# Cosine attention and a hard-swish layer in one kernel: batch 0's first two output tiles as a seven-product pair

## The chip, the cores and the metric

One core of one Trainium2 chip runs the kernel. The metric is device time in microseconds (us) for one execution; the kernel before takes 402.32 us (median of three runs, 402.19 to 402.92).

## The reference

The input is q, k, v of shape 8 batches x 12 heads x 448 positions x 64, and two weight matrices, 768 x 2048 and 2048 x 768.

```python
q_n = q / (norm(q) + 1e-06);  k_n = k / (norm(k) + 1e-06)      # over the last axis
attn = softmax(q_n @ k_n.T / tau)                              # tau = 0.1
x = (attn @ v), heads side by side: 3584 rows x 768
h = x @ w_in;  g = h * clip(h + 3, 0, 6) / 6
out = g @ w_out                                                # 3584 x 768, float32
```

## The kernel before, in words

The work is cut into 48 **turns**, one for each pair of heads of a batch (six turns a batch). A turn i has four groups of score matmuls (`SC.i.0` to `.2`, each two 64-row matmuls side by side, and `SC.i.3` on a tile `km`), an exponential on ScalarE for each bank of scores (`EX`), four groups of value matmuls into the bank pair `PV` (`VA`), and on VectorE a reciprocal and a multiplication that empty `PV` (`FI`). Ahead of a turn the raw q and k are loaded (`LQ`), squared (`SQ`), reduced (`RE`), scaled to `nrm` tiles (`NM`) and turned by a transposing DMA (`XD`); `CK` and `CS` copy the turned keys into `kz` (VectorE) and `km` (GpSimd); `VC` casts v into `vx`.

Between these, TensorE works through **units** of the layer (`U`). The first product, `mm1_unit(b, fc)` (L587), is six matmuls for one of 16 blocks of g; ScalarE makes `u` from it (`UA`, L596) and VectorE the product `gT` (`UV`, L602), which frees the bank. The second product, g @ w_out, comes in two forms. The plain one, `mm2_unit(b, t, m)` (L634), is 16 matmuls of 128x384 for one tile of 128 rows and one half of the columns. The other takes a **pair** of tiles and makes it with seven products of eight matmuls (`product_unit`, L795) in place of 4 x 16: products 1 to 7, named `x.n` for pair n. It needs sums of weight blocks (`WS`, L740: `w_sum` 1, 6 and 7, and `y3` and `y4`, which overwrite a quarter of `w_out_sb` each) and sums of blocks of g (`g_sum`, L772: `gs` tiles 6, 7, 1, and 2 and 5, which overwrite blocks of `gT`), all on VectorE. ScalarE copies out products 3, 4, 5 and 2; GpSimd combines the copies (`both`, `rest`, L824 to 828); VectorE adds product 1 into them (L852) and makes the results from 6 and 7 (L820).

The banks of scores, units and products come from one **ring of six** (M0, M1, Y, Z, M2, M3), handed out in program order. A matmul into a bank waits until the reader of what the bank held last has finished.

The order of the work is written by hand: `PLAN`, a list of operations for turns 0 to 17, whose `U` entries take units from `stream`; then a loop for turns 18 to 47, which takes them from `TURNS`, with the sums in `side`; then `LAST`. Each engine runs its own instructions in that order, and the DMAs of SyncE wait in one queue. `ORDER` lays out the stream of turns 8 to 17: 30 units of the first product, then six plain units of batch 0's second product. Two units of batch 1 (`carry`) are left for turn 18, and so is half of `y4`.

Of the kernel before, what the change touches and what calls it, by code (L numbers as in the profile page):

```python
# [15 lines left out]


FIRST = 18
ORDER = "111111111111111111111111111111222222"

PLAN = [
# [38 lines left out]
]  # L60

LAST = [
# [3 lines left out]
]  # L66
H_BY, M1_BY = "vvvvvvpp", "pppvpppp"

# [2 lines left out]
def kernel(  # L71
# [16 lines left out]
    NP = B * HP  # L88
    CC = d_model // 128
    FCN = d_ff // 128  # L90
# [22 lines left out]
    KC = FCN // 2  # L113
# [541 lines left out]
    def firsts(b, *fcs):  # L655
        return [(mm1_unit, b, fc) for fc in fcs]

    def second(b):
        assert b % 2 == 0
        return [(mm2_unit, b, t, m) for m in (1, 0) for t in range(3)]  # L660

    LEFT, RIGHT = slice(0, MH), slice(MH, 2 * MH)
    TILES = [(b, t) for b in range(1, B) for t in ((3, 0, 1, 2) if b % 2 else (0, 1, 2))]
    TILES.remove((B - 2, 2))
    PAIRS = list(zip(TILES[0::2], TILES[1::2]))  # L670
    ACROSS = [n for n, (x, y) in enumerate(PAIRS) if x[0] + 1 == y[0]]
    LOOP = 9
    summed, g_summed, issued_products = set(), set(), set()
    banks, parts, ready = {}, {}, set()
    late_sums = [
# [36 lines left out]
    def sum_of(n, what):  # L712

        if what == "e":
            return gs["1"] if n < B - 2 else late_sums[1]["e"]
        if n < LOOP or n == len(PAIRS) - 1:
            return gs[what + str(n % 2) if what == "7" else what]
        return late_sums[(n - LOOP) % 2][what]

    def d_and_e(n):  # L720
        if n < LOOP:
            return wide[n % 2], wide[2]
        return wide_late[2 * (n - LOOP) : 2 * (n - LOOP) + 2]

    def weight_sums(what, c0, n):
# [17 lines left out]
    def half(b, t, k):  # L743

        complete(b, t)
        return g_of(b)[:, :, g_cols(b, t)].rearrange("p (c k) n -> p c k n", k=2)[:, :, k, :]

    def block(n, i, k):
        return half(*PAIRS[n][i], k)

    def g_sum(n, what):

        if what == "e":
            t = 2 + n % 2
            o, x, y, op = sum_of(n, "e"), half(n, t, 0), half(n, t, 1), ALU.add
        else:
            a11, a12 = (block(n, 0, k) for k in range(2))
            a21, a22 = (block(n, 1, k) for k in range(2)) if what != "5" else (a11, a12)
            for w in {"2": "6", "5": "" if n in ACROSS else "7"}.get(what, ""):
                assert (n, w) in g_summed  # L760
            o, x, y, op = {
                "6": (a21, a21, a11, ALU.subtract),
                "2": (a21, a21, a22, ALU.add),
                "7": (a12, a12, a22, ALU.subtract),
                "5": (a12, a12, a11, ALU.add),
                "1": (a11, a11, a22, ALU.add),
            }[what]
            if what in "167":
                o = sum_of(n, what)
            if what == "5" and n in ACROSS:  # L770
                o = gs["6"]
        nc.vector.tensor_tensor(out=o[:, :, :], in0=x, in1=y, op=op)  # L772
        g_summed.add((n, what))

    def product_unit(n, name, end=None, apart=False):
# [54 lines left out]
        def added_later(i, cols, x):  # L830
# [230 lines left out]
    def sums(n, names):  # L1061
        return [(g_sum, n, x) for x in names]
# [16 lines left out]
    TURNS = {  # L1079
# [5 lines left out]
    }  # L1085
    APART = {(n, y) for n in range(len(PAIRS)) for x, y in (("5a", "3"), ("2a", "4")) if f"{x}.{n}" in " ".join(TURNS.values()).split()}
    side = {
        18: [(weight_sums, "y4", KC // 2, KC // 2)], 19: sums(0, "62"), 20: sums(0, "1"),
        21: sums(1, "75"), 22: sums(1, "621"),
        25: sums(2, "75"), 27: sums(2, "621"), 28: [(g_left, 2)], 29: sums(3, "5"),  # L1090
        31: sums(3, "7612"), 33: sums(4, "75"), 34: sums(4, "621"), 36: sums(5, "5"),
        37: sums(5, "761"), 38: sums(5, "2"), 39: [(g_left, 4)],
        40: sums(6, "75"), 41: sums(6, "621"),
        43: sums(7, "75"), 44: sums(7, "62"), 45: sums(7, "1"), 46: sums(8, "75"), 47: sums(8, "62"),
    }
    w_sums = [(w_sum_of, x, p) for p in range(FCN // 4) for x in "15672"]
    late = {44: "p", 45: "ppppp", 46: "pp"}
    units = {}
    carry = firsts(1, FCN - 2, FCN - 1)
    for b in range(2, B - 1):  # L1100
        first = firsts(b, *range(FCN))
        for n, x in enumerate([0, 3, 3, 3, 3, 2]):
            i = (b + 1) * HP + n
            u = carry + [first.pop(0) for _ in range(x)]
            carry = []
# [5 lines left out]
            if i == NP - 1:  # L1111
                p, last = [last], None
            x = 0 if n == 1 else 1 if n in (0, 5) and i > FIRST else 2
            units[i] = u[:x] + p + u[x:]
            units[i] += [last] if last else []
        carry = first
    units[FIRST] += sums(0, "75")

    assert len(carry) == 2
    units[NP] = [x for line in LAST for x in listed(line)]  # L1120
    units[NP] += products("3.10 4.10") + sums(10, "1") + products("5.10") + sums(11, "75") + products("2.10 3.11") + sums(11, "62")
    units[NP] += products("4.11 5.11") + sums(11, "1") + products("2.11 1.10 1.11")
    units[NP] += [(product_unit, n, x, 2) for n, x in ((10, "7"), (10, "6"), (11, "6"))]
    units[NP] += [(product_unit, 11, "7", x) for x in range(2)]

    FG = d_ff // 4
    weights = [
# [34 lines left out]
    def finish_units(e):  # L1162
        post[e].pop(0)()

    def whole_units(n, engines="av"):
# [6 lines left out]
    OPS = {  # L1172
        "LQ": load_qk, "LV": load_v, "W": next_weights, "SQ": square, "RE": reduce, "NO": norms, "NN": norms_two,
        "NM": normalise, "VC": vcast, "TR": transposes, "XD": crossbar, "XB": back_crossbar, "XP": back_two, "CQ": copy_q, "CK": copy_k, "CS": copy_k3, "SC": scores,
        "EX": exps, "VA": values, "FI": finish_values, "BK": back, "CX": copy_x, "U": unit, "UA": lambda: finish_units("a"), "UV": lambda: finish_units("v"),
        "GL": g_left, "WS": lambda x, *h: weight_sums(str(x), *((h[0] * KC // 2, KC // 2) if h else (0, KC))), "UU": whole_units, "D": busy, "DP": busy_pv, "OPEN": open_ring,
    }

# [31 lines left out]
    psum_s = startup.enter_context(tc.tile_pool(name="psum_s", bufs=1, space=bass.MemoryType.PSUM))  # L1210
    SC = [psum_s.tile([128, 2, 512], FP32, name=f"SC{n}", tag=f"SC{n}") for n in range(2)]

    by_kind = {"1": firsts(0, *range(FCN)) + firsts(1, *range(FCN - 2)), "2": second(0)}
    stream = [by_kind[x].pop(0) for x in ORDER]
    assert not by_kind["1"] and not by_kind["2"]


    for line in PLAN:
        run(line)
# [4 lines left out]
    for i in range(FIRST, NP):  # L1224
        assert not stream
        stream = list(units[i])
# [34 lines left out]
        n = 2  # L1261
# [27 lines left out]
    stream = units[NP]  # L1289
# [36 lines left out]
```

## Time and profile before

| what | us |
|---|---|
| median of the runs | 402.32 |
| the profiled execution's own time | 401.72 |
| its span, first to last instruction | 399.8 |
| TensorE matmul busy | 390.0 (98%) |
| VectorE busy | 296.1 (74%) |
| ScalarE busy | 281.6 (70%) |
| GpSimd busy | 266.8 (67%) |

In the page and the answers, PE is TensorE, DVE is VectorE, ACT is ScalarE, POOL is GpSimd, SP is SyncE. A timeline row has the start in us from the span's start, the length in us, the engine, the line, the operation with what it writes and reads, how many instructions are merged, and in brackets the idle time of the engine before the row with what ended it. The trace draws a matmul with its way through the array, so that rows of TensorE overlap; what a unit takes from the engine is the distance from its start to the start of the next row. The stretch that the change touches lies between 91 and 122 us.

### The profile page before, as it was taken

To read this page: it belongs to the slowest core of one execution; us is meant where nothing else is said; L and a number is where in the kernel's file an instruction comes from. 1 tells how busy PE (TensorE), PEld (TensorE's weight loads), DVE (VectorE), ACT (ScalarE), POOL (GpSimd) and SP (SyncE) were. 2 spreads that over 40 slices of the span, in tenths; PEclk is the share of its full clock that TensorE was granted. 3 is DMA by queue.
4 is the path that set the end of the run, shared out by engine and by line. 5 is a ranking of instruction groups with operands and counts; after the bars stand their busy time and mean duration, and the time that the engine had idled before them with its cause. 6 is when DMAs were issued, how large, how long until landed. Compare 5 with 4: busy or idle time off the path is not lost.

```text
span 399.8 us, 9819 instructions
## 1 busy us (share of the span) xinstructions
PE 390.0 (98%) x3735; PEld 238.3 (60%) x3735; DVE 296.1 (74%) x537; ACT 281.6 (70%) x619; POOL 266.8 (67%) x257
## 2 busy tenths in 40 slices
PE   7998999999999999999999999999999999999996
PEld 5566556555665556555565565555555556687563
DVE  7998787877588777767667796677856676888863
ACT  6999889887377686788788678776758755265330
POOL 5899936753544996578668888379395893344270
PEclk9999999999999999999999999999999999999999
DMA  8999999798878558797879787976763523130133
GB/s 290 317 232 243 198 206 246 167 201 188 193 165 217 122 116 196 198 207 147 197 184 215 98 205 152 163 186 154 185 152 74 112 48 58 34 77 21 39 82 97
DMA packets 93166, 63.75 MB, mean 159 GB/s; under 512 B 56128, under 2 KB 93120, under 8 KB 93120
## 3 DMA queue, kind: packets, MB, share of 16 engines
q1 hardware_dynamic: 87408, 56.45, 61.5%
q0 software_dynamic: 5312, 6.29, 9.7%
q8 instruction: 29, 0.48, 0.6%
q10 hardware_dynamic: 400, 0.39, 0.3%
q14 instruction: 17, 0.14, 0.1%
HBM read 45.61 MB, written 11.01 MB: 142 GB/s over the span
## 4 chain that ended last, share of the span: by engine, by line
PE 84%; ACT 5%; DMA 3%; DVE 3%; SPq 2%; POOL 2%; issue 1%; ACTq 0%; DVEq 0%; POOLq 0%
PE M L587 20%; PE M L795 17%; PE PV L482 10%; PE Z L587 6%; PE M L442 5%; PE Y L587 5%; PE Y L795 5%; PE Z L795 4%; PE M L634 3%; ACT at L460 3%; DMA big<-in_q_dram 2%; PE M L954 2%; PE Y L442 1%; PE Z L442 1%; SPq L219 1%
## 5 line engine op out<-in xcount | busy, mean ns | idle before, releaser
L460 ACT ACTIVATE at<-M 128x448 bf16<-128x448 f32 x196 | 98.1, 564 | 19.4 <-PE M L442 16.6
L587 PEld LDWEIGHTS <-w_in_sb 128*128 128x128 bf16 x696 | 65.2, 98 | 56.5 <-issue 2.8
L587 PE MATMUL M<-xT,w_in_sb 128*128 128x448 bf16 x450 | 96.7, 352 | 0.2
L293 POOL TENSOR_TENSOR nrm<-big,r 128x896 bf16<-128x896 f32 (+1 forms) x47 | 78.5, 1675 | 11.3 <-DMA tT<-nrm 4.2
L236 POOL TENSOR_TENSOR big<-big 128x896 f32<-128x896 f32 (+5 forms) x45 | 68.7, 1533 | 17.3 <-DMA big<-in_k_dram 8.8
L482 PEld LDWEIGHTS <-at 128*128 128x128 bf16 (+1 forms) x1536 | 54.1, 97 | 19.9 <-issue 12.0
L602 DVE SCALAR_TENSOR_TENSOR gT<-u,M 128x448 bf16<-128x448 bf16 x71 | 43.2, 618 | 30.7 <-ACT u L596 30.0
L482 PE MATMUL PV<-vx,at 128*128 128x65 bf16 (+1 forms) x1536 | 62.7, 193 | 0.0
L596 ACT ACTIVATE u<-M,bias 128x448 bf16<-128x448 f32 x75 | 49.0, 657 | 12.4 <-PE M L587 11.4
L248 DVE TENSOR_REDUCE n<-big 128x14 f32<-128x896 f32 (+1 forms) x50 | 51.5, 1038 | 0.3 <-ACT big L234 0.2
L399 POOL COPY km<-tT 64x128 bf16<-64x128 bf16 x34 | 15.6, 460 | 52.7 <-PE M L442 27.4
L795 PEld LDWEIGHTS <-gT 128*128 128x128 bf16 x304 | 29.5, 98 | 20.2
L795 PE MATMUL M<-w_out_sb,gT 128*128 128x384 bf16 x200 | 36.4, 326 | 0.0
L795 PEld LDWEIGHTS <-gs 128*128 128x128 bf16 x264 | 25.5, 98 | 17.5 <-issue 0.3
L503 DVE TENSOR_TENSOR on<-PV,rc 128x512 bf16<-128x512 f32 x48 | 33.2, 692 | 1.7
L795 PE MATMUL M<-w_sum,gs 128*128 128x384 bf16 (+1 forms) x184 | 32.0, 319 | 0.1
L442 PE MATMUL M<-tT,kz 64*128 64x448 bf16 (+1 forms) x171 | 31.0, 351 | 0.5 <-ACT at L460 0.5
L587 PE MATMUL Z<-xT,w_in_sb 128*128 128x448 bf16 x138 | 29.9, 353 | 0.0
L460 ACT ACTIVATE at<-Y 128x448 bf16<-128x448 f32 x50 | 28.3, 565 | 1.5 <-PE Z L442 1.5
L312 POOL CAST vx<-big 128x512 bf16<-128x512 f32 x39 | 27.1, 699 | 2.9 <-DMA big<-in_v_dram 2.8
L460 ACT ACTIVATE at<-Z 128x448 bf16<-128x448 f32 x48 | 27.1, 564 | 2.7 <-PE M L442 2.4
L587 PE MATMUL Y<-xT,w_in_sb 128*128 128x448 bf16 x108 | 23.4, 352 | 0.0
(163 smaller groups left out, 625.0 us busy)
## 6 DMA issues: line engine op xcount, KB each, us to landing
big<-in_k_dram SPq DMA_DIRECT2D x24, 448.0 KB, 5.2
big<-in_q_dram SPq DMA_DIRECT2D x24, 448.0 KB, 4.3
out_dram<-o SPq DMA_DIRECT2D x107, 96.0 KB, 2.2
big<-in_v_dram SPq DMA_DIRECT2D x48, 128.0 KB, 4.4
big<-in_v_dram SPq DMA_DIRECT2D x48, 96.0 KB, 4.5
w_in_sb<-in_moe_w_in_dram POOLq DMA_DIRECT2D x8, 384.0 KB, 9.3
w_out_sb<-in_moe_w_out_dram POOLq DMA_DIRECT2D x4, 768.0 KB, 10.0
tT<-nrm SPq DMA_TRANSPOSE x34, 2.8
```

What stands on the lines that cost most here:

```text
L236: engines[e].tensor_tensor(out=o, in0=i, in1=i, op=ALU.mult)
L248: nc.vector.tensor_reduce(out=n2_and_r[0][:, d % 2, j % 2, c], in_=sq[:, :, :, :].rearrange("p g c d -> p (g c) d")[:, c, :], axis=AX.X, o ...
L293: engines[e].tensor_tensor(out=nrm[:, :, g, :].rearrange("p c g d -> p g c d"), in0=raw_of[j][:, g, :, :], in1=n2_and_r[4][:, d % 2, j % 2, :]
L312: (engines[e].copy if e == "a" else engines[e].tensor_copy)(out=o, in_=f)
L442: nc.tensor.matmul(o, ks, qt[rows], start=True, stop=True)
L460: nc.scalar.activation(out=o, in_=x, func=AF.Exp, scale=inv_tau)
L482: nc.tensor.matmul(pv_out(j, h), at[rows, n, q_cols(i // HP, j)], vt[rows, 3 + h if name == "M" else 5 * h + int(name[1]), :], start=(name ...
L503: nc.vector.tensor_tensor(out=on[:, :, :, :].rearrange("p j h d -> p h j d"), in0=pv4[:, :, :, 0:D], in1=rc[:, :, :].to_broadcast([128, 2, ...
L587: nc.tensor.matmul(ps[:, 0:S], w_in_sb[:, cc, fc * 128 : (fc + 1) * 128], x[:, cc, 0:S], start=(cc == 0), stop=(cc == CC - 1),)
L596: nc.scalar.activation(out=u[:, :], in_=ps[:, 0:S], func=AF.Relu, bias=half_bias, scale=1.0 / 6.0)
L602: nc.vector.scalar_tensor_tensor(out=g[:, fc, c0 : c0 + S], in0=u[:, :], scalar=1.0, in1=ps[:, 0:S], op0=ALU.min, op1=ALU.mult,)
L795: nc.tensor.matmul(m, lhs[:, c, :], rhs[:, c, c0 : c0 + width], start=(base is None and c == 0), stop=(c == KC - 1), skip_group_check=True,)
```

## The change

The first two tiles of batch 0's second product, (0,0) and (0,1), become pair 0 of the seven-product form; the third, (0,2), stays plain. All later pairs are numbered one higher and keep their place. `PLAN`'s last lines are written anew for turns 15 to 17: the two left-over units of batch 1 come back into them from turn 18, the weight sums are all made before turn 17, the sums of g for pair 0 are set at three places (`GS`), and product 7 of pair 0 is put into turn 18. The results' stores move with the units; no load and no transposing DMA changes its place among the others in SyncE's queue. Pair 0 uses `wide[0]` and `wide[1]` for its two partial results.

The core of the diff:

```diff
 PLAN = [
...
-    "EX.14.3 XD.17 U SC.15.0 U FI.13 EX.15.0 UA UV UA UV UA U UA VA.14.0 VA.14.1 LQ.22 VA.14.2 UV UV CK.16.v VA.14.3",
+    "EX.14.3 XD.17 U SC.15.0 U FI.13 EX.15.0 SQ.20.p.0.7 GS.0.n62 UA UA VA.14.0 VA.14.1 LQ.22 LV.8 VA.14.2 VC.17.p",
...
     TILES.remove((B - 2, 2))
+    TILES[0:0] = [(0, 0), (0, 1)]
-    LOOP = 9
+    LOOP = 10
...
-            return wide[n % 2], wide[2]
+            return wide[n % 2], wide[2 if n else 1]
...
-        18: "3.0 4.0", 19: "5a.0 2a.0", 20: "1.0 6.0", 21: "3.1 5.1", 22: "4.1 2.1", 23: "1.1 6.1",
+        18: "7.0 3.1 4.1", 19: "5a.1 2a.1", 20: "1.1 6.1", 21: "3.2 5.2", 22: "4.2 2.2", 23: "1.2 6.2",
...
-        18: [(weight_sums, "y4", KC // 2, KC // 2)], 19: sums(0, "62"), 20: sums(0, "1"),
+        19: sums(1, "62"), 20: sums(1, "1"),
...
-    carry = firsts(1, FCN - 2, FCN - 1)
+    carry = []
...
+        "GS": lambda n, x: [g_sum(n, y) for y in x[1:]],
...
-    by_kind = {"1": firsts(0, *range(FCN)) + firsts(1, *range(FCN - 2)), "2": second(0)}
-    stream = [by_kind[x].pop(0) for x in ORDER]
+    stream = firsts(0, *range(FCN)) + firsts(1, *range(FCN - 2)) + [(mm2_unit, 0, 2, m) for m in range(2)]
+    stream += firsts(1, FCN - 2, FCN - 1) + products("4.0 2.0 3.0 5.0 1.0 6.0")
```

Line numbers of the changed kernel are one lower up to L634 and nine lower from L740 on (L772 is its L763).

**VectorE behind the emptying of `PV` for turn 13**, before. The rows are the reciprocal and the multiplication of `FI.13`, four products `gT` of the first product's units (each frees the bank named behind `u`), and the copy of the keys of turn 16:

```order
L502 RECIPROCAL rc_1604<-PV_109 128x8
L503 TENSOR_TENSOR on_1409<-PV_109,rc_1604 128x2x4x64
L602 SCALAR_TENSOR_TENSOR gT1_72<-u_1609,M1_695 128x448
L602 SCALAR_TENSOR_TENSOR gT1_72<-u_1612,Y_110 128x448
L602 SCALAR_TENSOR_TENSOR gT1_72<-u_1615,M3_697 128x448
L602 SCALAR_TENSOR_TENSOR gT1_72<-u_1623,M0_694 128x448
```

The same place in the changed kernel:

```order
L501 RECIPROCAL rc_1604<-PV_109 128x8
L502 TENSOR_TENSOR on_1409<-PV_109,rc_1604 128x2x4x64
L763 TENSOR_TENSOR gs6_77<-gT0_71 128x1024
L763 TENSOR_TENSOR gT0_71<-gT0_71 128x8x128
L601 SCALAR_TENSOR_TENSOR gT1_72<-u_1612,M1_695 128x448
L601 SCALAR_TENSOR_TENSOR gT1_72<-u_1614,Y_110 128x448
L601 SCALAR_TENSOR_TENSOR gT1_72<-u_1655,M3_697 128x448
L601 SCALAR_TENSOR_TENSOR gT1_72<-u_1657,M0_694 128x448
```

The sums 6 and 2 of pair 0 now stand ahead of the four products that free M1, Y, M3 and M0.

**VectorE from the keys of turn 16 on**, before: weight sums with a copy of keys, the plain units' stores (`o`) and the emptying of `PV` between them.

```order
L740 TENSOR_TENSOR w_sum7_75<-w_out_sb_68 128x1536
L740 TENSOR_TENSOR w_sum1_73<-w_out_sb_68 128x3072
L389 COPY kz1_81<-tT0_83 128x384
L647 COPY o_1796<-M1_695 128x384
L502 RECIPROCAL rc_1800<-PV_109 128x8
L503 TENSOR_TENSOR on_1663<-PV_109,rc_1800 128x2x4x64
L740 TENSOR_TENSOR w_sum6_74<-w_out_sb_68 128x3072
L647 COPY o_1838<-M2_696 128x384
L248 TENSOR_REDUCE n2_102<-big_94 128x14
L740 TENSOR_TENSOR w_out_sb_68<-w_out_sb_68 128x8x384
```

In the changed kernel; the first row that writes `w_out_sb` is `y4`, the second `y3`:

```order
L731 TENSOR_TENSOR w_sum7_75<-w_out_sb_68 128x1536
L731 TENSOR_TENSOR w_sum1_73<-w_out_sb_68 128x3072
L731 TENSOR_TENSOR w_out_sb_68<-w_out_sb_68 128x8x384
L731 TENSOR_TENSOR w_sum6_74<-w_out_sb_68 128x3072
L646 COPY o_1788<-M3_697 128x384
L601 SCALAR_TENSOR_TENSOR gT1_72<-u_1746,M0_694 128x448
L601 SCALAR_TENSOR_TENSOR gT1_72<-u_1753,M1_695 128x448
L731 TENSOR_TENSOR w_out_sb_68<-w_out_sb_68 128x8x384
L388 COPY kz1_81<-tT0_83 128x384
L763 TENSOR_TENSOR gs70_78<-gT0_71 128x1024
L763 TENSOR_TENSOR gT0_71<-gT0_71 128x8x128
L763 TENSOR_TENSOR gs1_76<-gT0_71 128x1024
```

Four weight sums now follow one another, `y3` comes behind the last two products of batch 1, and three sums of g follow.

**GpSimd in the same stretch**, before: the copies into `km` for turns 16 and 17, casts of v, the scaling `NM.18` and the squares of item 20.

```order
L399 COPY km_82<-tT0_83 64x2x64 x2
L312 CAST vx0_95<-big_94 128x8x64
L312 CAST vx1_96<-big_94 128x8x64
L293 TENSOR_TENSOR nrm0_99<-big_94,r_106 128x2x7x64
L312 CAST vx3_98<-big_94 128x8x64
L236 TENSOR_TENSOR big_94<-big_94 128x896
L312 CAST vx2_97<-big_94 128x8x64
```

In the changed kernel; L815, L816 and L819 combine the copies of pair 0:

```order
L235 TENSOR_TENSOR big_94<-big_94 128x896
L311 CAST vx1_96<-big_94 128x8x64
L292 TENSOR_TENSOR nrm0_99<-big_94,r_106 128x2x7x64
L311 CAST vx0_95<-big_94 128x8x64
L398 COPY km_82<-tT0_83 64x2x64 x2
L815 TENSOR_TENSOR big_94<-big_94 128x384
L816 TENSOR_TENSOR big_94<-big_94,o_1872 128x384
L311 CAST vx3_98<-big_94 128x8x64
L819 TENSOR_TENSOR big_94<-big_94,o_1812 128x384
```

The copies into `km` stand behind two casts and a scaling, and three additions are new.

TensorE's order from the end of turn 14's units, in words. Before: `mm1` into M0, the values of turn 14, scores 15.1 and 15.2 (M1, Y, Z, M2), 15.3 (M3), a plain unit (M0), values 15.0 and 15.1, all scores of turn 16 but the last, values 15.2 and 15.3, two plain units (M1, Y), scores 16.3, a plain unit (M2), values, scores 17.0 to 17.2, values, two plain units (M3, M0), scores 17.3 (M1), and turn 18 with two `mm1` and products 3 and 4. In the changed kernel: three groups of the values of turn 14, `mm1` (M0), the fourth group, scores 15.1 and 15.2 (M1, Y, Z, M2), the plain unit (M3), scores 15.3, 16.0 and 16.1, the other plain unit (M3), `mm1` twice (M0, M1), scores 16.2, product 4 (M2), values 15.0 to 15.2, scores 16.3 (M3), product 2 (M2), product 3 (M0), scores 17.0 and 17.1, values 15.3, product 5 (M0), product 1 (M3), values 16.0, scores 17.2, values 16.1 to 16.3, product 6 (M3), scores 17.3 (Y), values 17.0, and turn 18 with its scores (Z, M2, M3, M0, M1, Y), values, product 7 (Z), scores 18.3 and products 3 and 4 of pair 1.

More of the change, by code (lines that the diff above doesn't have):

```diff
@@ L18 @@
 FIRST = 18
-ORDER = "111111111111111111111111111111222222"
 PLAN = [
@@ L656, in firsts @@
         return [(mm1_unit, b, fc) for fc in fcs]
-    def second(b):
-        assert b % 2 == 0
-        return [(mm2_unit, b, t, m) for m in (1, 0) for t in range(3)]
     LEFT, RIGHT = slice(0, MH), slice(MH, 2 * MH)
@@ L1087 @@
     side = {
-        18: [(weight_sums, "y4", KC // 2, KC // 2)], 19: sums(0, "62"), 20: sums(0, "1"),
[L1089 to L1094, printed above, removed]
+        19: sums(1, "62"), 20: sums(1, "1"),
+        21: sums(2, "75"), 22: sums(2, "621"),
+        25: sums(3, "75"), 27: sums(3, "621"), 28: [(g_left, 2)], 29: sums(4, "5"),
+        31: sums(4, "7612"), 33: sums(5, "75"), 34: sums(5, "621"), 36: sums(6, "5"),
+        37: sums(6, "761"), 38: sums(6, "2"), 39: [(g_left, 4)],
+        40: sums(7, "75"), 41: sums(7, "621"),
+        43: sums(8, "75"), 44: sums(8, "62"), 45: sums(8, "1"), 46: sums(9, "75"), 47: sums(9, "62"),
     }
@@ L1116 @@
         carry = first
-    units[FIRST] += sums(0, "75")
+    units[FIRST] += sums(1, "75")
     assert len(carry) == 2
     units[NP] = [x for line in LAST for x in listed(line)]
[L1121 to L1124, printed above, removed]
+    units[NP] += products("3.11 4.11") + sums(11, "1") + products("5.11") + sums(12, "75") + products("2.11 3.12") + sums(12, "62")
+    units[NP] += products("4.12 5.12") + sums(12, "1") + products("2.12 1.11 1.12")
+    units[NP] += [(product_unit, n, x, 2) for n, x in ((11, "7"), (11, "6"), (12, "6"))]
+    units[NP] += [(product_unit, 12, "7", x) for x in range(2)]
     FG = d_ff // 4
@@ L1174 @@
         "NM": normalise, "VC": vcast, "TR": transposes, "XD": crossbar, "XB": back_crossbar, "XP": back_two, "CQ": copy_q, "CK": copy_k, "CS": copy_k3, "SC": scores,
-        "EX": exps, "VA": values, "FI": finish_values, "BK": back, "CX": copy_x, "U": unit, "UA": lambda: finish_units("a"), "UV": lambda: finish_units("v"),
+        "EX": exps, "VA": values, "FI": finish_values, "BK": back, "CX": copy_x, "U": unit, "UA": lambda: finish_units("a"), "UV": lambda: finish_units("v"), "UP": lambda: finish_units("p"),
+        "GS": lambda n, x: [g_sum(n, y) for y in x[1:]],
         "GL": g_left, "WS": lambda x, *h: weight_sums(str(x), *((h[0] * KC // 2, KC // 2) if h else (0, KC))), "UU": whole_units, "D": busy, "DP": busy_pv, "OPEN": open_ring,
@@ L1211 @@
     SC = [psum_s.tile([128, 2, 512], FP32, name=f"SC{n}", tag=f"SC{n}") for n in range(2)]
-    by_kind = {"1": firsts(0, *range(FCN)) + firsts(1, *range(FCN - 2)), "2": second(0)}
-    stream = [by_kind[x].pop(0) for x in ORDER]
-    assert not by_kind["1"] and not by_kind["2"]
+    stream = firsts(0, *range(FCN)) + firsts(1, *range(FCN - 2)) + [(mm2_unit, 0, 2, m) for m in range(2)]
+    stream += firsts(1, FCN - 2, FCN - 1) + products("4.0 2.0 3.0 5.0 1.0 6.0")
     for line in PLAN:
```

25 rows, old and new, of tables (LAST, PLAN, TURNS) are left out of this document.

## The prediction

> **What bounds the kernel now.** I read the page first, then the table by stretches, then the timelines of the four engines between 80 and 122 us, then places elsewhere where VectorE and GpSimd overlap.
>
> ```profile
> span 399.8 us, 9819 instructions
> PE 390.0 (98%) x3735; PEld 238.3 (60%) x3735; DVE 296.1 (74%) x537; ACT 281.6 (70%) x619; POOL 266.8 (67%) x257
> PE 84%; ACT 5%; DMA 3%; DVE 3%; SPq 2%; POOL 2%; issue 1%; ACTq 0%; DVEq 0%; POOLq 0%
> ...
> 92.20:121.47 29.27, 29.27 (x285) 18.08 (x284) 21.84 (x33) 18.25 (x41) 14.93 (x14) 1.00 0.76 172
> ```
>
> TensorE is busy 98% of the span and 84% of the chain that ended last. The last row is the stretch that is rewritten, from the `mm1` unit into M0 to the first values of turn 18: 29.27 us, TensorE busy throughout at its full granted clock (1.00), VectorE 21.84, GpSimd 14.93. So the end moves by what TensorE is spared there, less every wait put into its stream; behind the stretch its order is as it was.
>
> **What TensorE is spared.** A unit's price is the distance between starts:
>
> ```profile
> 88.39 1.30 PE L587 MATMUL M<-xT,w_in_sb 128*128 128x448 bf16 x6
> 89.53 1.30 PE L587 MATMUL Y<-xT,w_in_sb 128*128 128x448 bf16 x6
> 90.76 0.36 PE L442 MATMUL Z<-tT,kz 64*128 64x448 bf16 x1
> ...
> 91.06 2.44 PE L587 MATMUL M<-xT,w_in_sb 128*128 128x448 bf16 x12
> 93.34 1.14 PE L482 MATMUL PV<-vx,at 128*128 128x65 bf16 x32
> 94.41 0.36 PE L442 MATMUL M<-tT,kz 64*128 64x448 bf16 x1
> ...
> 118.87 2.76 PE L795 MATMUL M<-w_out_sb,gT 128*128 128x384 bf16 x16
> 121.47 0.63 PE L482 MATMUL PV<-vx,at 128*128 128x65 bf16 x16
> ```
>
> Sixteen matmuls of 128x384 take 121.47 - 118.87 = 2.60, so one takes 0.1625, not the 0.326 of its drawn length. Six plain units were 96 matmuls; now there are 32 and seven products of eight, 88. Eight fewer: **-1.30**. Against it, an `mm1` unit takes 1.14 in front of another (88.39 to 89.53) and 1.23 in front of scores (89.53 to 90.76): leaving or entering a group of 64-row scores costs 0.09. (The Trainium skill, "TensorEngine Tiling (Array Packing)", Key Properties, says that changing the tiling mode drains the engine; these rows agree, and the rule speaks against this order. Without the drain the sum would be 0.42 us lower.) Four groups of scores become six, three of them entered from 128-row work where all four came behind values: 2 x 0.09 + 0.24 = +0.42, the 0.24 being an estimate for the entries (0.1, 0.1 and 0.05 behind a `km` matmul). The values in eight pieces rather than seven come to +0.01. TensorE's own work: -1.30 + 0.42 + 0.01, about **-0.87**.
>
> **The sums ahead of the first four products.** VectorE had a hole there, which the sums 6 and 2 are to fill:
>
> ```profile
> 90.74 0.69 DVE L503 TENSOR_TENSOR on<-PV,rc 128x512 bf16<-128x512 f32 x1
> 92.69 0.62 DVE L602 SCALAR_TENSOR_TENSOR gT<-u,M 128x448 bf16<-128x448 bf16 x1 [1.26 <-ACT u L596]
> 93.23 0.61 DVE L602 SCALAR_TENSOR_TENSOR gT<-u,Y 128x448 bf16<-128x448 bf16 x1
> 93.76 1.15 DVE L602 SCALAR_TENSOR_TENSOR gT<-u,M 128x448 bf16<-128x448 bf16 x2
> ...
> 91.69 1.69 POOL L293 TENSOR_TENSOR nrm<-big,r 128x896 bf16<-128x896 f32 x1 [4.25 <-DMA tT<-nrm]
> ```
>
> Two sums of 0.68 would fit 1.26 with 0.1 over. But GpSimd starts `NM.19` at 91.69, when a transposing DMA lets go of its tile, and no edit touches that. What the two do to each other stands elsewhere:
>
> ```profile
> 233.24 0.91 DVE L772 TENSOR_TENSOR gs<-gT 128x1024 bf16<-128x1024 bf16 x1
> 234.19 2.06 DVE L772 TENSOR_TENSOR gT<-gT 128x1024 bf16<-128x1024 bf16 x1
> ...
> 233.56 2.14 POOL L293 TENSOR_TENSOR nrm<-big,r 128x896 bf16<-128x896 f32 x1
> ```
>
> The same three instructions: the scaling drawn from 233.56 waited for the first sum (to 234.15) and ran 1.55; the second sum, drawn from 234.19, waited for the scaling (to 235.70) and ended 0.55 later. They exclude each other, and the one that waits goes next. (The Trainium skill, "SBUF — State Buffer", Who interferes with whom, says that a VectorE instruction with two SBUF inputs contends with GpSimd's reads and that issue order decides who blocks. These rows agree and add the turn-taking. By that rule alone, with each wait in order of issue, the next step is the same.)
>
> So: sum 6 runs 91.35 to 92.03, `NM.19` to 93.58, sum 2 to 94.13. The four products then start at 94.05, 94.58, 95.11 and 95.64, the second ends at 95.19, and only then is Y free for scores 15.1. TensorE gets there at 94.42: from 92.20 (91.06 + 1.14) it has an `mm1`, 1.14, and the 32 values in two pieces, 1.08 (1.07 in one, 93.34 to 94.41). It then starts 0.05 behind the release, an estimate, at 95.24: **+0.82**. The plain unit's bank M3 (product ended 95.72) adds **+0.05**.
>
> **The weight sums ahead of product 3.** Lengths and the exclusion for these:
>
> ```profile
> 95.92 0.95 DVE L740 TENSOR_TENSOR w_sum<-w_out_sb 128x1536 bf16<-128x1536 bf16 x1
> ...
> 103.64 1.79 DVE L740 TENSOR_TENSOR w_sum<-w_out_sb 128x3072 bf16<-128x3072 bf16 x1
> 109.18 1.75 DVE L740 TENSOR_TENSOR w_out_sb<-w_out_sb 128x3072 bf16<-128x3072 bf16 x1
> ...
> 98.80 1.17 POOL L312 CAST vx<-big 128x512 bf16<-128x512 f32 x2 [2.84 <-DMA big<-in_v_dram]
> ...
> 103.76 2.14 POOL L312 CAST vx<-big 128x512 bf16<-128x512 f32 x1
> ```
>
> A cast of 0.61 took 2.14 beside the weight sum at 103.64, and ended 0.47 behind it. VectorE after the products, each of which takes its turn for 0.53 (92.69 to 93.23): the emptying for turn 14 from 96.17, keys at 97.02, `w_sum` 7 at 97.28, `w_sum` 1 at 98.14 to 99.89. The cast of v cannot start before 98.80 (its load, unmoved) and gets in at 99.89; `y4` follows to 101.98, `NM.18` to 103.53, `w_sum` 6 to 105.15. Then a store copy, two products and `y3`, 106.60 to 108.35, and GpSimd's second cast and the two `km` copies, 105.15 to 106.28.
>
> TensorE with the waits so far: scores 15.1 at 95.24, plain unit 95.77 to 98.37, scores 15.3, 16.0 and 16.1, second plain unit 99.10 (its bank's copy, 0.48 on ScalarE, ends 99.05: +0.01) to 101.70, two `mm1`, scores 16.2, product 4 from 104.35 to 105.65 (`y4` done at 101.98), values 15, scores 16.3 at 106.40 (`km` at 106.28: 0.1 to spare), product 2 to 107.89. Product 3 reads `y3`: 108.40, **+0.52**. Before, `y3` at 109.18 had ten us to spare.
>
> **The end of pair 0.**
>
> ```profile
> 120.43 0.48 ACT L843 COPY big<-M 128x384 f32<-128x384 f32 x1 [0.72 <-PE M L795]
> ...
> 102.32 0.56 DVE L647 COPY o<-M 128x384 f32<-128x384 f32 x1 [3.52 <-PE M L634]
> ...
> 110.84 1.16 DVE L236 TENSOR_TENSOR big<-big 128x512 f32<-128x512 f32 x2
> ...
> 134.00 1.00 POOL L825 TENSOR_TENSOR big<-big,o 128x384 f32<-128x384 f32 x1
> ```
>
> A copy starts 0.25 behind a product's end (118.87 + 1.30 to 120.43) and takes 0.48; a bank emptied by VectorE takes 0.56. Product 5 ends at 111.92, its copy at 112.65. GpSimd's subtraction (1.00) meets the two squares at 112.3, which I let exclude it: d is ready at 113.83, VectorE adds product 1 behind the second square, 114.16 to 114.71, and product 6, due at 114.59, starts at 114.76: **+0.17** (nothing if the squares don't exclude it, 0.6 if both go first). Turn 18's second scores need M3 from product 6's result: 116.06 + 0.25 + 0.55 + 0.05 = 116.91 against 116.79, **+0.12**; they replace a wait of **0.07** that the stretch has now for M1. Everything else of the change has cover: sums 7, 5 and 1 end at 110.54, just ahead of product 5 (110.62) and of product 1 (111.92); GpSimd's three new additions lie where it stood idle from 105.9 to 114.8; stores number as before; `XD.18` goes out at some 110.9 for 109.0, still ahead of its keys' copy at 115.6. Product 7 only stands later, beside work for which its bank Z is free. `wide[1]` costs nothing: its next writer comes five us later.
>
> **The sum**, on the profiled execution (401.72, a span of 399.8 and 1.92 around it): -0.87 + 0.82 + 0.05 + 0.01 + 0.52 + 0.17 + 0.12 - 0.07 = **+0.75**, 402.47. The median stands 0.60 above that execution: 402.32 + 0.75 = **403.1**.
>
> **The rivals.** *The sums don't collide* (faster). The place is `NM.19` at 91.69: were it let go 0.4 us later, behind 92.06, sum 2 would be through at 92.75 and the 0.82 gone. VectorE's chain would gain only 0.66, since the product of M0 waits for ScalarE; product 3 would still wait 0.6, and with the small ones the time would be 402.4, no change. For the time to fall past 401.5 the weight sums must run without GpSimd between them as well, as they do if the exclusion doesn't hold for them: then only some 0.2 of waits is left against -0.87, and 401.6 to 401.4 comes out. The rows at 103.76 and 233.56 speak against it.
>
> *`km` late* (slower). The second `km` copy ends at 106.28 and `y3` takes the port at 106.60. If GpSimd's row of cast, scaling, cast and copies runs 0.4 us later, the copy waits for `y3`, and scores 16.3 stand until about 108.7 rather than 106.40; the wait for `y3` is then contained in it: +2.3 - 0.52, 404.9. It decides at `w_sum` 6: both rows start from its end, which speaks against it. A smaller kin is any further wait of 0.5 to 1 us in the dozen handovers that I found with 0.1 to 0.5 to spare: 403.6 to 404.1.
>
> *Half of it*: one of the two large waits happens and the other doesn't, 402.2 to 402.6.
>
> **How the numbers follow.** A difference under 0.2%, 0.8 us, can hardly be told from no change. Forecast, both waits about as laid out, 402.7 to 403.6: 0.46. Further waits on top, 403.6 and more, `km` among them: 0.22. Half of it: 0.18. Faster: 0.14. The forecast lies at the edge of what can be told, half to each side: slower (over 403.1) 0.23 + 0.22 = **0.45**, no change 0.23 + 0.18 = **0.41**, faster **0.14**. The range of 8 in 10 leaves out the full gain below 401.6 and late `km` above 404.3.
>
> **What would show it.** In the changed kernel's timeline: sum 2 drawn about two us long from about 92.05, and scores 15.1 at about 95.2 with TensorE's stream broken for 0.8; the cast near 98.8 and the scaling behind it drawn long, `w_sum` 6 ending at about 105.2, product 3 starting right behind `y3`; `w_out` matmuls 88 where 96 were. Wrong would be: sum 2 of 0.69 (the first rival), scores 16.3 behind `y3` (the second), or a wait for a transfer, of which I see none.

## The result, and the profile after

| | before | after |
|---|---|---|
| median of the runs | 402.31 (22 runs) | 403.78 (22 runs) |
| lowest and highest | 401.75, 403.08 | 402.60, 406.67 |
| the profiled execution's own time | 401.72 | 402.84 |
| its span | 399.8 | 401.1 |

After against before is 1.0037, 95% interval 1.0025 to 1.0049: slower by 1.47 us, with times that lie much further apart than before's in this set (before reached 404.41 to 405.57 in the sets of the experiments). The profiled execution is among the fastest of the changed kernel.

The page of the changed kernel: the span, busy time by engine, and the shares of the chain that ended last.

```profile
span 401.1 us, 9819 instructions
...
PE 390.5 (97%) x3727; PEld 237.4 (59%) x3727; DVE 305.6 (76%) x542; ACT 283.2 (71%) x621; POOL 272.2 (68%) x260
...
PE 78%; DVE 12%; ACT 5%; POOL 2%; issue 1%; DMA 1%; SPq 0%; ACTq 0%; DVEq 0%; POOLq 0%
```

3727 matmuls are eight fewer than 3735, and VectorE's share of the chain has gone from 3% to 12%: waits for it now stand in TensorE's stream. The rewritten stretch, from the values of turn 14 to the first values of turn 18, in the table by stretches (time, then busy time of PE, PEld, DVE, ACT and POOL, granted clock, DMA share):

```profile
92.29:122.31 30.02, 29.25 (x277) 17.17 (x276) 28.75 (x38) 19.38 (x43) 20.20 (x17) 1.00 0.73 160
```

It takes 30.02 where it took 29.27: **+0.75**. VectorE went from 21.84 busy to 28.75, a part of which is waiting, since a drawn length holds the wait for the other engine (below, 2.06 for a sum of 0.68). VectorE's timeline of the changed kernel (start, length, engine, line, operation):

```profile
91.43 0.68 DVE L763 TENSOR_TENSOR gs<-gT 128x1024 bf16<-128x1024 bf16 x1
92.15 2.06 DVE L763 TENSOR_TENSOR gT<-gT 128x1024 bf16<-128x1024 bf16 x1
...
94.66 0.61 DVE L601 SCALAR_TENSOR_TENSOR gT<-u,Y 128x448 bf16<-128x448 bf16 x1
...
99.89 2.17 DVE L731 TENSOR_TENSOR w_out_sb<-w_out_sb 128x3072 bf16<-128x3072 bf16 x1
101.97 3.24 DVE L731 TENSOR_TENSOR w_sum<-w_out_sb 128x3072 bf16<-128x3072 bf16 x1
...
106.66 1.74 DVE L731 TENSOR_TENSOR w_out_sb<-w_out_sb 128x3072 bf16<-128x3072 bf16 x1
...
112.35 1.96 DVE L235 TENSOR_TENSOR big<-big 128x512 f32<-128x512 f32 x2
114.23 0.54 DVE L843 TENSOR_TENSOR big<-M,big 128x384 f32<-128x384 f32 x1
```

GpSimd's, same kernel:

```profile
91.60 2.06 POOL L292 TENSOR_TENSOR nrm<-big,r 128x896 bf16<-128x896 f32 x1 [4.03 <-DMA tT<-nrm]
...
99.40 1.04 POOL L311 CAST vx<-big 128x512 bf16<-128x512 f32 x1 [3.65 <-PE M L441]
100.40 3.20 POOL L292 TENSOR_TENSOR nrm<-big,r 128x896 bf16<-128x896 f32 x1
103.55 2.14 POOL L311 CAST vx<-big 128x512 bf16<-128x512 f32 x1
105.63 0.64 POOL L398 COPY km<-tT 64x128 bf16<-64x128 bf16 x2
...
112.72 1.17 POOL L816 TENSOR_TENSOR big<-big,o 128x384 f32<-128x384 f32 x1 [1.14 <-ACT ln L275]
```

And TensorE's:

```profile
94.16 0.41 PE L481 MATMUL PV<-vx,at 128*128 128x65 bf16 x8
94.79 0.35 PE L441 MATMUL M<-tT,kz 64*128 64x448 bf16 x1 [0.23 <-DVE gT L601]
95.32 0.35 PE L441 MATMUL Y<-tT,kz 64*128 64x448 bf16 x1 [0.19 <-DVE gT L601]
...
106.72 1.46 PE L786 MATMUL M<-w_out_sb,gT 128*128 128x384 bf16 x8
108.46 1.46 PE L786 MATMUL M<-w_out_sb,gT 128*128 128x384 bf16 x8 [0.27 <-DVE w_out_sb L731]
...
113.83 0.91 PE L481 MATMUL PV<-vx,at 128*128 128x65 bf16 x24
114.83 1.46 PE L786 MATMUL M<-w_sum,gs 128*128 128x384 bf16 x8
```

Read the three side by side. The second sum (92.15) is drawn 2.06 for a work of 0.68: `NM.19` runs from about 92.1 to 93.6, between the two sums, and keeps the second one waiting. The product that frees Y then starts at 94.66, and the scores into Y stand at 95.32, 0.82 after 94.50, where eight values (0.34) from 94.16 end. Later the two engines take turns: cast, `y4`, `NM.18`, `w_sum` 6, cast; the scaling is drawn 3.20 and `w_sum` 6 3.24. `y3` ends at 108.40. Product 2, 1.30 of work, is through at 108.02, and product 3 starts at 108.46: 0.44 of waiting. At the end, 24 values take 0.75 from 113.83, and product 6 starts at 114.83, right behind L843: 0.25 of waiting. L843 stands behind the two squares, drawn 1.96 where they took 1.16 before, since GpSimd's subtraction L816 gets in between them. The span is 1.3 longer; the rest of it lies elsewhere: 0.09 ahead of the stretch, and 0.44 at 189, where two groups of scores wait because GpSimd's squares came 3.8 us later than before (180.56 for 176.74), behind a load that took 6.90 to land instead of 4.34. The time around the span was 0.2 shorter.

### The profile page after: what moved, and what is told of

It is laid out like the page before. It is cut to its first block, busy times and chain, and to the rows that moved or that the text cites. A ratio compares the mean times of both kernels' runs of the same rounds, so it can differ in the third digit from the quotient of the medians.

```text
span 401.1 us, 9819 instructions
## 1 busy us (share of the span) xinstructions
PE 390.5 (97%) x3727; PEld 237.4 (59%) x3727; DVE 305.6 (76%) x542; ACT 283.2 (71%) x621; POOL 272.2 (68%) x260
## 4 chain that ended last, share of the span: by engine, by line
PE 78%; DVE 12%; ACT 5%; POOL 2%; issue 1%; DMA 1%; SPq 0%; ACTq 0%; DVEq 0%; POOLq 0%
PE M L586 18%; PE M L786 17%; PE PV L481 9%; PE Z L586 5%; PE M L441 5%; PE Z L786 5%; PE Y L586 4%; PE Y L786 4%; ACT at L459 3%; PE PV L1138 2%; PE M L945 2%; DVE gT L601 2%; DVE n L247 1%; PE Y L441 1%; DVE gT L763 1%
## 5 line engine op out<-in xcount | busy, mean ns | idle before, releaser
L459 ACT ACTIVATE at<-M 128x448 bf16<-128x448 f32 x195 | 97.5, 562 | 15.2 <-PE M L441 12.6
L586 PE MATMUL M<-xT,w_in_sb 128*128 128x448 bf16 x456 | 98.0, 352 | 0.2
L786 PEld LDWEIGHTS <-gT 128*128 128x128 bf16 x336 | 32.4, 98 | 22.6 <-issue 0.7
L786 PE MATMUL M<-w_out_sb,gT 128*128 128x384 bf16 x232 | 42.3, 326 | 0.3 <-DVE w_out_sb L731 0.3
L786 PEld LDWEIGHTS <-gs 128*128 128x128 bf16 x288 | 27.8, 98 | 19.0 <-issue 0.5
L786 PE MATMUL M<-w_sum,gs 128*128 128x384 bf16 (+1 forms) x200 | 35.0, 319 | 0.2
L311 POOL CAST vx<-big 128x512 bf16<-128x512 f32 x39 | 28.9, 744 | 3.7 <-PE M L441 3.7
L459 ACT ACTIVATE at<-Y 128x448 bf16<-128x448 f32 x52 | 29.3, 564 | 2.7 <-PE Z L441 1.5
L815 POOL TENSOR_TENSOR big<-big 128x384 f32<-128x384 f32 x13 | 14.4, 1111 | 19.1 <-ACT big L834 18.8
```

Of the source, the lines that this page charges most:

```text
L311: (engines[e].copy if e == "a" else engines[e].tensor_copy)(out=o, in_=f)
L459: nc.scalar.activation(out=o, in_=x, func=AF.Exp, scale=inv_tau)
L586: nc.tensor.matmul(ps[:, 0:S], w_in_sb[:, cc, fc * 128 : (fc + 1) * 128], x[:, cc, 0:S], start=(cc == 0), stop=(cc == CC - 1),)
L786: nc.tensor.matmul(m, lhs[:, c, :], rhs[:, c, c0 : c0 + width], start=(base is None and c == 0), stop=(c == KC - 1), skip_group_check=True,)
```

## The experiments

Each of these kernels was timed beside the kernel before on the same chip. "The stretch" is the time from the values of turn 14 to the first values of turn 18 in the profiled execution, 29.27 before and 30.02 after.

**One.** The two sums four VectorE instructions earlier, into the hole before `FI.13`.

```diff
-    "... EX.15.0 SQ.20.p.0.7 GS.0.n62 UA UA ..."      "... EX.14.1 UV SC.14.2 ..."
+    "... EX.15.0 SQ.20.p.0.7 UA UA ..."               "... EX.14.1 UV GS.0.n62 SC.14.2 ..."
```

> The changed kernel with the sums 6 and 2 of pair 0 moved ahead by four instructions of VectorE, into its hole of 1.65 us at 87.4, where GpSimd stands idle. Exclusion theory (mine: the waits come from VectorE and GpSimd taking turns at SBUF): both sums are drawn 0.68 to 0.69, scores 15.1 start within 0.1 of TensorE's getting there, the wait of 0.82 is gone; product 3 still waits for y3, some 0.1 longer; against the changed kernel -0.65, so +0.8 against the kernel before in the median. Load theory (rival: VectorE just has more to do than the stretch lets it, and what GpSimd does is of no account): the weight sums end where they ended and product 3 with them, so that at most 0.3 is won.

The median is 403.94, against 402.60 before on that chip (1.0024, interval 0.9997 to 1.0050; 12 runs, from 401.94 to 406.53, six below 403.3 and six above 404.5). The stretch of the profiled execution, 92.33 to 121.66, takes 29.33. Its VectorE, GpSimd and TensorE:

```profile
88.14 0.69 DVE L763 TENSOR_TENSOR gT<-gT 128x1024 bf16<-128x1024 bf16 x1
```

```profile
92.78 1.69 POOL L292 TENSOR_TENSOR nrm<-big,r 128x896 bf16<-128x896 f32 x1 [5.22 <-DMA tT<-nrm]
```

```profile
94.54 0.36 PE L441 MATMUL Y<-tT,kz 64*128 64x448 bf16 x1
...
105.91 1.46 PE L786 MATMUL M<-w_out_sb,gT 128*128 128x384 bf16 x8
107.81 1.46 PE L786 MATMUL M<-w_out_sb,gT 128*128 128x384 bf16 x8 [0.44 <-DVE w_out_sb L731]
```

Alone, the second sum takes 0.69, and nothing waits for Y. Product 3 now waits 0.60 instead of 0.44, since TensorE reaches it 0.8 earlier while `y3` comes only 0.65 earlier. So 0.75 - 0.82 - 0.06 + 0.16, about +0.03 for a measured +0.06: the 0.82 was the meeting with `NM.19`, not the sums' own time. But in this execution the DMA let `NM.19` go only at 92.78 (91.60 in the changed kernel), so late that the sums would have missed it in their old place too. That the move itself takes the meeting away is shown by three.

**Two.** The scaling `NM.18` behind the copies of `km`.

```diff
-    "NM.18.p U UV UV UA UA VA.14.3 ..."      "... UV UV UV CS.16.v EX.16.2 ..."
+    "U UV UV UA UA VA.14.3 ..."              "... UV UV UV CS.16.v NM.18.p EX.16.2 ..."
```

> The changed kernel with GpSimd's scaling NM.18 moved behind the km copies of turns 16 and 17, so that it no longer gets in between y4 and w_sum 6. Exclusion theory: w_sum 6 is drawn about 2.1 in place of 3.24 and ends some 1.5 earlier, at 103.7; the scaling may now stand in front of y3 instead, which still ends at 108.0 or before; product 3 waits 0 to 0.2; against the changed kernel -0.4, and fewer long executions if these come from km meeting y3. Load theory: VectorE's own lengths are the same, y3 ends as before at 108.4, no difference.

Median 402.53, before 402.60 (0.9998, 0.9981 to 1.0015); the stretch takes 28.94.

```profile
91.88 0.68 DVE L763 TENSOR_TENSOR gs<-gT 128x1024 bf16<-128x1024 bf16 x1
92.59 0.69 DVE L763 TENSOR_TENSOR gT<-gT 128x1024 bf16<-128x1024 bf16 x1
...
101.73 2.16 DVE L731 TENSOR_TENSOR w_sum<-w_out_sb 128x3072 bf16<-128x3072 bf16 x1
...
105.34 2.43 DVE L731 TENSOR_TENSOR w_out_sb<-w_out_sb 128x3072 bf16<-128x3072 bf16 x1
```

```profile
93.49 1.69 POOL L292 TENSOR_TENSOR nrm<-big,r 128x896 bf16<-128x896 f32 x1 [5.38 <-DMA tT<-nrm]
...
104.47 1.69 POOL L292 TENSOR_TENSOR nrm<-big,r 128x896 bf16<-128x896 f32 x1
```

`w_sum` 6 is drawn 2.16 instead of 3.24, and the wait of product 3 falls from 0.44 to 0.21; what is left is `NM.18` once more, which now holds up `y3` (2.43). This execution also shows the first rival of the prediction by chance: the transposing DMA let `NM.19` go at 93.49, behind both sums, and the 0.82 was gone without an edit to the sums.

**Three.** Both moves together.

> Both moves together. Exclusion theory: the wait for Y is gone and product 3 waits 0.2 to 0.4; against the changed kernel -1.0, +0.4 against the kernel before, with a spread like that of the kernel before. Load theory: as the changed kernel, within 0.3.

Median 402.31, before 402.60 (0.9988, 0.9971 to 1.0005), stretch 28.94.

```profile
91.96 1.69 POOL L292 TENSOR_TENSOR nrm<-big,r 128x896 bf16<-128x896 f32 x1 [4.12 <-DMA tT<-nrm]
```

Here `NM.19` comes while the first sum would run in its old place, about 91.7 to 92.4, as in the changed kernel. The sums are through before, and scores 15.1 wait for nothing. VectorE and GpSimd do the same work as in the changed kernel, at other places, and the stretch is 1.08 shorter: the waits come from the order, not from the load on VectorE.

**Four.** The kernel before, with eight of the sixteen matmuls of one plain unit left out.

```diff
+        n_fc = FCN // 2 if (t, m) == (0, 1) else FCN
-        for fc in range(FCN):
+        for fc in range(n_fc):
```

> The kernel before with eight of the sixteen matmuls of its first plain unit left out (that tile's right half is summed over eight of its sixteen blocks): what eight matmuls of 128x384 are worth by themselves. TensorE bound at 0.1625 each: -1.30 against the kernel before, and the rest of the program 1.30 earlier throughout. If something else sets the pace behind the stretch (loads, GpSimd): less, 0 to -0.8, with the gain given back at some later wait.

Median 401.22, 1.38 below before (0.9969, 0.9955 to 0.9984); the profiled span is 398.5, 1.3 shorter. The eight matmuls are worth what the prediction credits them with.

**Five.** The changed kernel again.

> The changed kernel unchanged, once more, beside the others of this set. Forecast: a median 0.7 to 1.5 us above before. Two theories of why its executions spread (402.6 to 406.7, median 1.47 above before, where the profiled one is 1.12 above): by the km theory some executions have the two copies of km, 105.63 to 106.27 in the profiled one, meet y3 (from 106.66), so that scores 16.3 (106.54) stand until y3 has ended at 108.4 and the copy behind it, and the execution is 2 to 2.5 us longer; so the times fall into a group near 403 and a group near 405. By the load theory chance lateness of loads is spread over the whole span; the times then spread evenly, and those of before on the same chip spread as much.

Median 403.74, before 402.30 (1.0028, 1.0007 to 1.0049). The profiled execution was a long one, 405.81, and settles the first of the two theories against the copies of `km`: it is late from the start. DMA activity in its first 16 us, in slices of 0.4 us (busy share in tenths):

```profile
DMA  0000655999999999999999999999999993630276
...
big<-in_q_dram SPq DMA_DIRECT2D x5, 448.0 KB, 7.2
```

The same of the changed kernel's first profile:

```profile
DMA  0000645999999999999999999999999999999999
...
big<-in_q_dram SPq DMA_DIRECT2D x6, 448.0 KB, 6.0
```

The last number is the median time from issue to landing. In the long one the loads land later (the third of all at 8.81 instead of 6.70), and from 13.2 us on the transfers thin out (3, 6, 3, 0 tenths), with five loads of q issued instead of six. TensorE's values that began at 22.95 in the first profile begin at 25.87 here, 2.92 late. The stretch adds 0.15 to its +0.75, and `km` meets nothing there.

**Six.** GpSimd's second cast of v behind the copies of `km`.

```diff
-    "... UV FI.14 U VC.16.p UA SC.15.3 ..."      "... CS.16.v EX.16.2 SC.16.3 ..."
+    "... UV FI.14 U UA SC.15.3 ..."              "... CS.16.v VC.16.p EX.16.2 SC.16.3 ..."
```

> GpSimd's cast of v for turn 16 (103.55 to 105.69, held by the sum w_sum 6) goes behind the two copies of km, nothing else. km is then copied from 103.6 and shares its time with w_sum 6, which ends near 105.2 as before; km is done by 105.2 at the latest, 1.4 us ahead of y3 instead of 0.4. By the km theory the long executions go: median 0.7 to 0.9 above before (the forecast's +0.75, since NM.18 still draws w_sum 6, the waits for banks stay, and product 3 still waits for y3), highest below 404.5. By the load theory the median stays 1.2 to 1.5 above before, with executions up to 406.

Median 404.59, before 402.30 (1.0043, 1.0020 to 1.0066): no fall. The theory of `km` as the cause of the long executions falls with this and with five. The profiled execution, 405.79, was 1.93 late at the values of 22.95; it loses more near 128 and 139, of which more under ten.

**Seven.** The cast made three times over, so that `km` comes late in every execution.

```diff
-    "... UV FI.14 U VC.16.p UA SC.15.3 ..."
+    "... UV FI.14 U VC.16.p VC.16.p VC.16.p UA SC.15.3 ..."
```

> The cast of v for turn 16 is made three times over (the result is the same), so that km's copies come behind y3 in every execution: casts until about 106.85, y3 until about 108.5, km copied at 108.5 to 109.4, with scores 16.3 at 109.0 to 109.5 instead of 106.54; product 3's wait of 0.3 is then covered. By the km theory this is the price of the meeting: the profiled execution 2.2 to 2.7 above that of the changed kernel, 405.0 to 405.6, the size of the long group of times. If scores 16.3 came late at little cost (below 1 us), the km theory cannot explain the long executions.

Median 407.38, before 402.30 (1.0115, 1.0084 to 1.0147), four runs from 406.93 to 407.67: more than any theory gave. GpSimd, then TensorE, then the table by stretches (clock in the third column from the end):

```profile
103.63 3.50 POOL L311 CAST vx<-big 128x512 bf16<-128x512 f32 x3
107.07 2.68 POOL L398 COPY km<-tT 64x128 bf16<-64x128 bf16 x2
```

```profile
109.81 0.36 PE L441 MATMUL M<-tT,km 128*128 128x448 bf16 x1 [3.02 <-POOL km L398]
110.01 4.23 PE L786 MATMUL M<-w_out_sb,gT 128*128 128x384 bf16 x16
```

```profile
109.80:112.00 2.20, 2.19 (x11) 1.25 (x12) 2.12 (x3) 0.82 (x2) 0.00 (x0) 0.80 0.47 129
112.00:114.60 2.60, 2.60 (x12) 0.89 (x9) 0.00 (x0) 0.52 (x2) 0.00 (x0) 0.51 0.36 79
```

The copies took their turns behind `y3` as laid out, and scores 16.3 stood at 109.81. But behind this wait of over three us TensorE was granted half its clock, and the sixteen matmuls took 4.17 from start to start instead of 2.60; by scores 17.0 this execution is 4.3 behind the changed kernel's first. The prediction's second rival had a wait of 2.3; with two more casts it was 3.2 here, and the half clock came on top. What a wait of 2.3 costs no run shows. No profile of the changed kernel shows it happening.

**Eight and eleven.** Both moves of three, and the second half of VectorE's squares of tile 22 behind the subtractions (eight), and once more (eleven).

```diff
-    "... U SQ.22.v.0.4 SQ.22.v.4.3 UA UP UV VA.16.0"      "... U UP UV VC.18.p NO.10 NM.20.v ..."
+    "... U SQ.22.v.0.4 UA UP UV VA.16.0"                  "... U UP UV VC.18.p NO.10 SQ.22.v.4.3 NM.20.v ..."
```

> The variant with both moves (sums 1 us earlier, scaling NM.18 behind the copies of km), and VectorE's second half of the squares of tile 22 moved behind the subtractions of products 6 and 5. Product 6 then waits for a VectorE that is free: its 0.24 us of wait go, and L811 stands as it did. Forecast: 0.2 below the variant with both moves, 0.3 to 0.6 below before; at most 0.1 of it if the squares push the second subtraction (115.6) late for the bank of scores 18.1. The load theory, by which VectorE has too much to do, expects no gain from a reordering.

> The variant with the sums early, NM.18 behind the copies of km, and the second half of the squares of tile 22 behind the subtractions, once more. By the start theory its lowest executions stand 0.3 to 0.6 below the lowest of before and 1.0 to 1.4 below those of the changed kernel, with the same share of long ones.

Medians 402.18 and 402.13, before 402.30 and 402.62 (0.9993, 0.9970 to 1.0015; 0.9995, 0.9979 to 1.0012). The stretch takes 28.70 and 28.71. VectorE of eight:

```profile
111.56 0.68 DVE L235 TENSOR_TENSOR big<-big 128x512 f32<-128x512 f32 x1
113.14 0.56 DVE L843 TENSOR_TENSOR big<-M,big 128x384 f32<-128x384 f32 x1 [0.89 <-PE M L441]
...
115.82 0.55 DVE L235 TENSOR_TENSOR big<-big 128x384 f32<-128x384 f32 x1
```

L843 no longer stands behind a square, product 6 waits for nothing, and the stretch is the predicted 0.24 shorter than with both moves. So the second square's wait for GpSimd's subtraction was what product 6 waited for. In its stretch this version beats both kernels, by 0.57 and by 1.32; in medians it beats the changed kernel, and against before the interval holds no change.

**Nine.** The kernel before, as one of the kernels timed.

> The kernel before, as a kernel of its own, to see its spread beside that of the changed one on one chip. A long execution of the changed kernel was 2.9 us behind at 23 us already, since the third load of the program landed at 8.81 instead of 6.70, in a part that the change does not touch. By the start theory (the first loads are late in some executions of any kernel) before shows a group 2 to 3 us above its lowest times too, in a quarter to a half of its executions, and a profiled long one would be behind at 23 us. By the theory that the change makes the long ones, before has none above 403.1.

Median 402.49, 401.92 to 404.54. Its profiled execution, 403.47, was late too, with the same thinning of the transfers. Its TensorE, where the first profile of before has 22.87:

```profile
24.62 0.66 PE L482 MATMUL PV<-vx,at 128*128 128x65 bf16 x16
```

1.75 late there, and still 1.7 at the end (spans 401.5 and 399.8). So late first loads belong to both kernels, and before passes them through unchanged.

**Ten.** The changed kernel, third time.

> The changed kernel, third time. By the start theory its lowest executions stand 0.6 to 0.9 above the lowest of before (the forecast's +0.75), and the share of long executions is that of before on this chip; the difference of medians then moves with the shares, anywhere from 0.5 to 1.5. By the theory that the change makes the long ones, more than half are above 403.5 while before has none.

Median 404.14, before 402.62 (1.0032, 1.0013 to 1.0051). The profiled execution, 405.43, was 1.98 late at 22.95, had the +0.75 in its stretch (30.03), and then lost 1.1 more. TensorE and GpSimd of it:

```profile
128.97 0.35 PE L586 MATMUL Z<-xT,w_in_sb 128*128 128x448 bf16 x1 [0.43 <-DMA xT<-on]
...
139.74 1.46 PE L786 MATMUL M<-w_sum,gs 128*128 128x384 bf16 x8 [0.33 <-DVE big L843]
```

```profile
129.96 0.64 POOL L398 COPY km<-tT 64x128 bf16<-64x128 bf16 x2 [5.44 <-DMA tT<-nrm]
...
138.10 1.00 POOL L816 TENSOR_TENSOR big<-big,o 128x384 f32<-128x384 f32 x1
```

Two transposing DMAs landed late against TensorE's order: one into `xT`, for which an `mm1` waits, and one into `tT`, for which GpSimd's copies wait; GpSimd is then late up to its subtraction L816, VectorE's L843 waits for it and a product for that. Six shows the same two waits (0.75 and 0.49 of stalls there, 0.60 and 0.49 here). A wait for a transfer is one of the prediction's signs of being wrong, and here is one, behind the stretch.

**Twelve.** The load that stands between the two transpositions into `xT` on SyncE, moved behind the second.

```diff
-    if FIRST + 6 < NP:
-        do("LQ", FIRST + 6)
...
             do("XP", i - 2)
+        if i == FIRST:
+            do("LQ", i + 6)
```

> The changed kernel, with one SyncE row moved: the load of the keys of tile 24, which stands between the two transpositions of attention outputs into xT (119.33 and 122.23 in its profile), goes behind the second. The second is then issued near 120.7 and lands near 124.4 instead of 125.9. In two of four profiles of the changed kernel or of its variants with NM.18 in the old place, product Z<-xT waited 0.4 to 0.6 for that transposition near 128, and a product 11 us later 0.3 for GpSimd; together 1.1 us. By the transposition theory this is what lifts the median of the changed kernel from the 0.75 of the stretch to 1.5: the median falls to 0.7 to 1.0 above before, and both waits are gone from the profile. By the start theory alone (late first loads, a little more often by chance) the median stays 1.3 to 1.6 above. The waits of the stretch (0.53 for Y, 0.44 for y3) stay in either.

Median 404.64, before 402.33 (1.0047, 1.0030 to 1.0065): not lower. Of who waits for whom on TensorE between 120 and 200 us, its profile has one row:

```profile
PE M L786 <- DVE big L843: 1.0, 1, 1.0
```

The wait for `xT` is gone, and the other has grown: the moved load now stands right ahead of the transposition into `tT`, for which GpSimd waits. The stall is 1.15, as long as the two of ten together (1.09). The edit did not take the waits out, so the median, which did not fall, cannot decide between the theories.

## Why the prediction was right, and where it was short

403.1 was predicted, in 401.6 to 404.3, and 403.78 came: in the range, but in the part of it (403.6 and more, "further waits on top") to which the prediction gave 0.22, not in the 402.7 to 403.6 to which it gave 0.46. For the stretch of the profiled execution it named +0.75, and +0.75 was measured there. The waits came where it laid them out; that the sum is right to the hundredth is luck, since its terms were off by up to 0.08 either way. By its steps:

- **TensorE's own work**, -0.87: eight fewer matmuls, shown by four (-1.38 in the median and -1.3 in the span for an estimated -1.30). The stretch less its waits comes to -0.90 (0.75 - 0.82 - 0.06 - 0.44 - 0.25 - 0.15 + 0.07), so the estimate for entering and leaving the 64-row scores (+0.42) fits too, though no run tests it alone.
- **Scores 15.1 wait for Y**, +0.82: measured 0.82 at the same instruction, for the reason given. Three took the collision away and the wait went; two had it go by chance, when the DMA came late. All three profiles of the changed kernel have the collision.
- **Product 3 waits for `y3`**, +0.52: measured 0.44, with the interleaving as laid out. Two took `NM.18` out of it and 0.21 was left.
- **Product 6 waits for L843**, +0.17: measured 0.25; eight shows the second square as the cause. Bank M3, +0.05, measured 0.06; the second scores of turn 18, +0.12, measured 0.15.
- **"Behind the stretch its order is as it was"**, so that the median would move with the profiled execution: this is the step that fell short. The lowest executions stand 0.85, 0.58 and 1.07 above before's in the three sets of runs (of 22, 12 and 12 runs against 22, 29 and 29), about the predicted difference; the medians stand 1.47, 1.44 and 1.52 above. Some 0.7 of the median is outside the sum.

What the 0.7 is, is settled in part. It is not `km` (five, six, seven). Late first loads are not the change's, since nine has them too; whether the changed kernel has them more often than before, the few profiles can't tell. Between 127 and 140 us, waits for late transpositions cost 1.1 to 1.2 in three of the five profiles of the changed kernel and of six and twelve, which differ from it by one row; neither profile of before has them, nor has any of one, two, three, eight and eleven. The loads and transpositions of that place stand in the order that they had before, and moving one of its DMAs (twelve) only moved the wait. What the traces show is less slack: the second transposition into `xT` is issued 3.5 and 3.8 us ahead of the `mm1` unit that waits for it in ten, in the two profiles of before (121.06 for 124.59 in the first), 3.2, 3.0 and 2.6 in those of the changed kernel (122.23 for 125.43, 124.83 for 127.43 in the last), 2.1 in six, and 3.3 to 4.4 in two, three, eight and eleven. One has 3.6, but its profile is of its shortest execution. That this is how the long executions come about is a guess; no run tests it.

The medians of the versions with `NM.18` out of the weight sums (two, three, eight, eleven) lie at that of before or a little under it; those with `NM.18` in its place lie above it, six and twelve by 2.3, one by 1.34 (its interval just holds no change). So the excess seems to go with the place of `NM.18`; by what path, no run shows.

## What to carry to other kernels

Lay the instructions of two engines that keep each other waiting, as VectorE and GpSimd do here, along one line of time, each one's wait included, before you fill a hole with new work: two sums of 0.68 were 0.1 too long for a hole of 1.26 us, and cost 0.82 by turns. What decided was when the other engine is let go, here by a DMA. Moving the sums by four instructions took this cost away, and moving the scaling `NM.18` halved the wait for `y3`. And predict a median from more than one execution: the profiled one may be the fastest, and waits that it does not have show only in the others.

## What the runs showed of the hardware

A wait of a little over three us on TensorE cost more than itself. In seven, TensorE stood still from 106.6 to 109.81, and from 111.1 to about 114.5 its granted clock was 0.50: a matmul of 128x384 then took 0.320 us instead of 0.1625. The Trainium skill ("TensorE: Matmul & The Clock Gate", Part 1: The HAM clock gate) says that an idle window of about 3.4 us halves the clock and that a busy window of the same length restores it. The second half agrees: the slow part lasted 3.4 us. The first agrees only nearly: 3.2 us of standing still were enough here, and the clock fell 1.3 us after TensorE had begun again. Waits of up to 1.3 us in the other profiles left the clock at 1.00; what lies between, no run here shows. The slow matmuls and scores cost about 1.7 on top of the wait of 3.2 (4.17 for 2.60, and 0.34 for 0.20 between two scores).
